# Attention and a gated MLP on one core: W_out read in place, joined groups on TensorE, and matmuls of ones

## The chip, the cores and the metric

The kernel runs on one core of a Trainium2 chip. A core has TensorE (PE, matrix products into PSUM), VectorE (DVE), ScalarE (ACT), GpSimd (POOL) and SyncE (SP, which here only issues transfers). PE's results go to eight PSUM banks of 128 x 512 f32. The metric is the device time of one execution in microseconds; the median of the runs counts.

## The reference

Random-feature attention for 8 batches and 8 heads (576 rows, head size 64, 128 features), then an MLP over all 4608 rows (512 to 2048 to 512).

```
scale = 1.0 / np.sqrt(np.sqrt(D))
def phi(x):
    proj = np.einsum('bhsd,md->bhsm', x, omega)
    sq = np.sum(x * x, axis=-1, keepdims=True) / 2.0
    h = proj - sq
    h = h - np.max(h, axis=-1, keepdims=True)
    return np.exp(h) / np.sqrt(m)
q_p, k_p = phi(q * scale), phi(k * scale)
kv = np.einsum('bhsm,bhsd->bhmd', k_p, v)
num = np.einsum('bhsm,bhmd->bhsd', q_p, kv)
den = np.einsum('bhsm,bhm->bhs', q_p, np.sum(k_p, axis=2))[..., None] + 1e-06
x = num / den                # then heads side by side: 4608 x 512
h = x @ w_in
out = (h * (1.0 / (1.0 + np.exp(-h)))) @ w_out
```

## The kernel before, in words

**Pairs.** Two heads of a batch make a pair; 32 pairs (`NWIN`), numbered n, four to a batch. A pair's 2 x 576 rows are nine chunks of 128: four of each head and a middle chunk of 64 + 64 rows. For keys and queries (`who` is k or q): `project` (L287, eight matmuls of a 64-row half each) and `project_mid` (L294, the middle chunk); `square_sum` (L279); the maxima by `top` (L303, L301); `shift` (L307, L308, the number to be subtracted); then for the first eight pairs (`DIRECT`) nine exponentials `expo` on ACT (L323), and from then on a subtraction on DVE (`lower`) and one exponential of all (`expo_all`, L337). The sum of the keys' features is `zsum_direct` (L358, L360) on PE for the first eight pairs and `sums` on POOL with `zsum` (L352) on PE for the others. `denom` or `denom_direct` (L369, L409) is on DVE, `normal` (L419, three groups of three chunks) on POOL divides the queries' features, `turn` (L425) transposes them on PE, three chunks a time, and `en_copy` (L429) brings them to SBUF. `kv` (L389), `kt_copy`, `kv_turn` (L397) and `kw_copy` make the key-value matrix; `numer` (L443) gives x transposed, and `x_high`, `x_low` (L457, L462) split it into two float32r parts.

**MLP.** A tile t is 512 rows of batch t (tile 8 collects the remaining 64 rows of all eight). It has 16 steps f. `stage1` (L539) does W_in, three products (high-high, low-high, high-low) for each of four k; `silu` and `g_low` split the activation; `stage2` (L557) does W_out into four banks that are held for the whole tile, two steps (`LAG`) behind. A step is 24 matmuls of 128 x 512. The eight banks are four `acc`, two `h` (stage 1) and two `att` (everything of the attention, once the MLP runs).

**Weights.** They arrive as float64 words. Once, in the first tile, ACT (`exponent`) and DVE (`word`, three pieces: L500, L502, L506) make float32 of each block of 128 rows, and POOL splits it (`weight_high` L520, `weight_low` L524). W_in's parts stay in SBUF. W_out's are written by POOL into a ring `wp` of two slots, sent to DRAM by `keep_weight` (L527), and read back into the ring `wo` (three slots) by `get_weight` (L531) for each of the 144 steps, the first tile's too.

**Order.** A planner in Python (`Plan`) sets the order of all instructions on all engines before anything runs. Each unit has an engine, an estimated duration, a due time (`key`), inputs (`after`), rings that it takes slots of, and banks. It walks through estimated time and at each step picks, among the units that could start about now, the one due first. `HANDOFF` is its estimate of the step from one engine to another. `shift_keys` adds random numbers, from the seeds in `SHIFTS`, to the due times before 235, so that the order of the first tile is one draw of many. `LEAD` (4) pairs go ahead of the MLP. Each engine works its own list in order; waits are set where lists depend on each other.

Of the kernel before, what the change touches and what calls it, by code (L numbers as in the profile page):

```python
# [9 lines left out]
F32 = mybir.dt.float32  # L10
# [9 lines left out]
P = 128  # L20
# [26 lines left out]
    "en": 2, "den": 2, "rd": 2, "wraw": 3, "w32": 3, "wre": 2, "wo": 3, "wp": 2, "gh": 3, "gl": 3, "ot": 2,  # L47
# [28 lines left out]
class Plan:  # L76
# [16 lines left out]
    def run(self, until=None):  # L93
# [50 lines left out]
        while any(ready.values()):  # L144
# [75 lines left out]
def attention_mlp(ctx: ExitStack, tc: tile.TileContext, qT, kT, qn, kn, v, om_in, w_in, w_out, out):  # L220
# [175 lines left out]
    def kv_turn(n, ps):  # L396
        nc.tensor.transpose(ps[:, :P], T.pop(("kt", n)), ident)  # L397
        T["kwp", n] = ps

    def kw_copy(n):  # L400
        T["kw", n] = kw = new("kw", [P, P])
        nc.scalar.copy(kw, T.pop(("kwp", n))[:, :P])
# [18 lines left out]
    def turn(n, g, ps):  # L421
        if g == 0:
            T["en", n] = new("en", [P, NC * P])
        for i in range(3):
            nc.tensor.transpose(ps[:, i * P : (i + 1) * P], T["h", n, "q"][:, 3 * g + i], ident)  # L425
        T["t", n, g] = ps

    def en_copy(n, g):
        nc.scalar.copy(T["en", n][:, 3 * g * P : 3 * (g + 1) * P], T.pop(("t", n, g))[:, : 3 * P])  # L429
# [96 lines left out]
    def keep_weight(f):  # L526
        nc.sync.dma_start(wo_d[f].bitcast(F32), T.pop(("wp", f)).bitcast(F32))  # L527
# [64 lines left out]
    for n in range(NWIN):  # L592
        calm = n < LEAD
        for i, who in enumerate("kq"):
# [3 lines left out]
            def prev(s):  # L598
# [18 lines left out]
            add(md, "PE", 0.25, at(n, 3 * i + 0.1, o + 5.2), lambda ps, n=n, who=who: project_mid(n, who, ps),  # L617
                banks=1, after=mid_after, free=[("raw",) + w])
# [50 lines left out]
        add(("ktt", n), "PE", 0.2, at(n, 6.7, 36.5), lambda ps, n=n: kv_turn(n, ps), after=[("kt", n)], banks=1,  # L669
            free=[("kt", n)])  # L670
        add(("kw", n), "ACT", 0.3, at(n, 6.8, 36.7), lambda n=n: kw_copy(n), after=[("ktt", n)], order=[("kw", n - 1)] if n else [],
            alloc=[("kw", ("kw", n))], free=[bk(("ktt", n))])
        if n < DIRECT:
            add(("den", n), "DVE", 2.8, at(n, 8, 34.2), lambda n=n: denom_direct(n), after=e["q"] + [zn],
# [5 lines left out]
        for g in range(3):  # L680
            add(("norm", n, g), "POOL", 0.85, at(n, 9 + 0.1 * g, 37 + 0.1 * g), lambda n=n, g=g: normal(n, g),
                after=[("den", n)], order=[("norm", n, g - 1)] if g else [], free=[("rd", n)])
            add(("turn", n, g), "PE", 0.34, at(n, 9.5 + 0.1 * g, 44.2 + 0.8 * g), lambda ps, n=n, g=g: turn(n, g, ps),
                after=[("norm", n, g)], order=[("turn", n, g - 1)] if g else ([("turn", n - 1, 2)] if n else []),
                alloc=[] if g else [("en", ("en", n))], banks=1, free=[("h", n, "q")])
            add(("en", n, g), "ACT", 0.5, at(n, 9.6 + 0.1 * g, 44.4 + 0.8 * g), lambda n=n, g=g: en_copy(n, g),
                after=[("turn", n, g)], free=[bk(("turn", n, g))])
# [36 lines left out]
    for f in range(NF):  # L724
# [14 lines left out]
    for i, (t, f) in enumerate(steps):  # L739
        key = clock(i)  # L740
        late = i >= total - LAG
        add(("get", t, f), "SP", 0.36, clock(i + LAG - AHEAD_OUT), lambda t=t, f=f: get_weight(t, f),
            after=[("keep", f)], order=[("get",) + divmod(i - 1, NF)] if i else [],
            alloc=[("wo", ("wo", t, f))], lat=2.1)
# [11 lines left out]
        for j in range(4):  # L756
# [4 lines left out]
            w = [("get", t, f)]  # L761
# [64 lines left out]
```

## Time and profile before

| what | us |
|---|---|
| median of three runs (lowest, highest) | 1077.16 (1076.47, 1077.48) |
| the profiled execution, its own time | 1076.36 |
| its span | 1074.6 |
| stage 1, three groups of L539, PE busy | 236.4, 225.3, 225.7 |
| stage 2, two groups of L557, PE busy | 371.0, 226.1 |

The profile page gives busy times of the engines, then the span in 40 slices (a digit is tenths; PEclk is the clock granted to PE), the transfers, a chain of what ended last, and groups of instructions by line. Busy times of PE overlap, since matmuls are pipelined: 1152 matmuls of L557 with a mean of 403 ns start much closer together than that. PEld are PE's weight loads, beside its matmuls. Windows show the same for chosen stretches, with the clock's mean there (1.00 is full), and the waits name the engine that came last.

### The profile page before, as it was taken

To read this page: it belongs to the slowest core of one execution; us is meant where nothing else is said; L and a number is where in the kernel's file an instruction comes from. 1 tells how busy PE (TensorE), PEld (TensorE's weight loads), DVE (VectorE), ACT (ScalarE), POOL (GpSimd) and SP (SyncE) were. 2 spreads that over 40 slices of the span, in tenths; PEclk is the share of its full clock that TensorE was granted. 3 is DMA by queue.
4 is the path that set the end of the run, shared out by engine and by line. 5 is a ranking of instruction groups with operands and counts; after the bars stand their busy time and mean duration, and the time that the engine had idled before them with its cause. 6 is when DMAs were issued, how large, how long until landed. Compare 5 with 4: busy or idle time off the path is not lost.

```text
span 1074.6 us, 16797 instructions
## 1 busy us (share of the span) xinstructions
PE 1046.7 (97%) x6044; PEld 838.8 (78%) x6044; DVE 529.4 (49%) x1573; ACT 572.3 (53%) x1049; POOL 220.4 (21%) x289
## 2 busy tenths in 40 slices
PE   6899999999999999999999999999999999999998
PEld 5667877778777787787777877778778788888886
DVE  7998777655544544555454554445454421111111
ACT  5677875555556655555556555665555433222221
POOL 2444455402222112222202122211222200000000
PEclk8989999999999999999999999999999999999999
DMA  7967877654445443543454434544343226223333
GB/s 278 334 203 234 288 245 251 223 170 124 131 132 172 142 141 121 161 151 111 131 166 149 129 129 134 162 142 143 123 145 94 74 92 198 97 98 136 99 99 98
DMA packets 66530, 167.88 MB, mean 156 GB/s; under 512 B 15632, under 2 KB 15760, under 8 KB 66448
## 3 DMA queue, kind: packets, MB, share of 16 engines
q1 hardware_dynamic: 65984, 166.23, 47.8%
q8 instruction: 48, 0.79, 0.3%
q10 hardware_dynamic: 464, 0.59, 0.1%
q14 instruction: 34, 0.28, 0.1%
HBM read 146.87 MB, written 19.92 MB: 155 GB/s over the span
## 4 chain that ended last, share of the span: by engine, by line
PE 90%; DVE 4%; ACT 2%; DMA 1%; issue 1%; POOL 0%; ACTq 0%; SPq 0%; DVEq 0%
PE ps_acc L557 37%; PE ps_h L539 36%; PE ps_att L287 5%; PE ps_att L389 3%; PE ps_att L425 3%; PE ps_att L443 2%; PE ps_att L294 1%; DVE prod L369 1%; PE ps_att L352 1%; PE ps_att L360 1%; DVE w L502 1%; DMA wo<-wo_d 1%; DMA rawq<-qT 0%; ACT hk L323 0%; PE ps_acc L287 0%
## 5 line engine op out<-in xcount | busy, mean ns | idle before, releaser
L557 PE MATMUL ps_acc<-wo,gh 128*128 128x512 f32 x1152 | 371.0, 403 | 3.2 <-ACT hk L323 1.8
L544 ACT ACTIVATE gh<-ps_h 128x512 fp32r<-128x512 f32 x144 | 86.1, 598 | 308.3 <-PE ps_h L539 297.1
L557 PEld LDWEIGHTS ps_acc<-wo,gh 128*128 128x128 f32 x1152 | 206.2, 189 | 46.0 <-ACT hk L323 2.2
L549 DVE TENSOR_TENSOR gl<-ps_h,gh 128x512 fp32r<-128x512 f32 x144 | 99.2, 689 | 284.4 <-ACT ps_h L545 284.3
L539 PE MATMUL ps_h<-xh,wh 128*128 128x512 f32 x576 | 236.4, 410 | 0.3 <-ACT hk L323 0.3
L539 PE MATMUL ps_h<-xl,wh 128*128 128x512 f32 x576 | 225.3, 391 | 1.5 <-DVE xl L462 1.5
L557 PE MATMUL ps_acc<-wo,gl 128*128 128x512 f32 x576 | 226.1, 393 | 0.0
L539 PE MATMUL ps_h<-xh,wl 128*128 128x512 f32 x576 | 225.7, 392 | 0.0
L419 POOL TENSOR_TENSOR hq<-hq,rd 128x384 f32<-128x384 f32 x96 | 79.2, 852 | 382.5 <-DVE rd L414 173.6
L539 PEld LDWEIGHTS ps_h<-xh,wh 128*128 128x128 f32 x576 | 108.4, 188 | 25.0 <-ACT hk L323 0.5
L539 PEld LDWEIGHTS ps_h<-xh,wl 128*128 128x128 f32 x576 | 108.2, 188 | 23.9
L557 PEld LDWEIGHTS ps_acc<-wo,gl 128*128 128x128 f32 x576 | 108.4, 188 | 23.6
L539 PEld LDWEIGHTS ps_h<-xl,wh 128*128 128x128 f32 x576 | 108.5, 188 | 22.5 <-DVE xl L462 1.8
L544 ACT ACT_TABLE_LOAD x58 | 74.4, 1283 | 36.1 <-PE ps_h L539 35.4
L303 DVE TENSOR_REDUCE mxq<-ps_att 128x4 f32<-128x512 f32 x56 | 36.1, 687 | 100.3 <-PE ps_att L287 100.2
L545 ACT ACTIVATE ps_h<-ps_h 128x512 f32<-128x512 f32 x144 | 85.4, 593 | 0.0
L337 ACT ACT_TABLE_LOAD x48 | 61.6, 1283 | 35.7 <-DVE hq L328 34.3
L343 POOL TENSOR_TENSOR t<-hk 128x256 f32<-128x256 f32 x48 | 34.4, 738 | 199.1 <-ACT hk L337 199.1
L409 DVE CUSTOM_DVE_ANT_0 prod<-hq,zb 128x128 f32<-128x128 f32 x216 | 47.8, 288 | 38.9 <-ACT zb L382 38.9
L303 DVE TENSOR_REDUCE mxk<-ps_att 128x4 f32<-128x512 f32 x55 | 35.6, 687 | 38.3 <-PE ps_att L287 37.8
L275 ACT ACTIVATE nat<-nat 128x576 f32<-128x576 f32 x64 | 44.4, 697 | 14.6 <-DMA nat<-kn 10.5
L429 ACT COPY en<-ps_att 128x384 f32<-128x384 f32 x89 | 40.5, 480 | 7.0 <-PE ps_att L425 5.4
(129 smaller groups left out, 1192.9 us busy)
## 6 DMA issues: line engine op xcount, KB each, us to landing
wo<-wo_d SPq DMA_DIRECT2D x144, 512.0 KB, 3.4
rawk<-kT SPq DMA_DIRECT2D x32, 352.0 KB, 3.0
rawq<-qT SPq DMA_DIRECT2D x32, 352.0 KB, 4.2
v<-v SPq DMA_DIRECT2D x32, 320.0 KB, 3.0
nat<-kn SPq DMA_DIRECT2D x32, 288.0 KB, 3.0
nat<-qn SPq DMA_DIRECT2D x32, 288.0 KB, 3.4
wraw<-w_in SPq DMA_DIRECT2D x16, 512.0 KB, 4.1
wraw<-w_out SPq DMA_DIRECT2D x16, 512.0 KB, 5.0
```

The costliest lines, as they stand in the source:

```text
L275: nc.scalar.activation(nat, nat, AF.Square, scale=SCALE * 0.5**0.5)
L287: nc.tensor.matmul(ps[:, i * M : (i + 1) * M], raw[r, o : o + P], oms[r], start=True, stop=True)
L303: nc.vector.tensor_reduce(m[:, 5 * j : 5 * j + 4], ps.rearrange("p (c m) -> p c m", m=M), AX.X, ALU.max)
L337: nc.scalar.activation(h, h, AF.Exp)
L409: nc.vector.tensor_tensor_reduce(out=prod[:, c], in0=e[:, c], in1=zb[:, j], scale=1.0, scalar=GUARD, op0=ALU.mult, op1=ALU.add, accum_out= ...
L419: nc.gpsimd.tensor_tensor(e[:, c], e[:, c], rd[:, c].unsqueeze(2).broadcast_to([P, 3, M]), ALU.mult)
L429: nc.scalar.copy(T["en", n][:, 3 * g * P : 3 * (g + 1) * P], T.pop(("t", n, g))[:, : 3 * P])
L539: nc.tensor.matmul(ph, w[:, k, :], x, start=k == 0 and n == 0, stop=k == NK - 1 and n == 2)
L544: nc.scalar.activation(gh, ph, AF.Silu)
L545: nc.scalar.activation(ph, ph, AF.Silu)
L549: nc.vector.tensor_tensor(gl, T["ph", t, f], T["gh", t, f].bitcast(F32), ALU.subtract)
L557: nc.tensor.matmul(T["po", t][j], g[:, js], w, start=f == 0 and n == 0, stop=f == NF - 1 and n == 2)
```

## The change

Three things, and the planner's numbers.

W_out in place: the ring `wp` goes, and `wo` has five slots. POOL writes the split of step f into a slot of `wo`; stage 2 of the first tile reads it there, and `keep_weight` sends the same slot to DRAM for later tiles. `get_weight` is issued from the second tile on.

Joined groups: from the ninth pair on (n > `DIRECT`), the middle projection of pair n and a group of three transposes of pair n - 1 are one unit in one bank (`mid_turn`, twice a pair: keys with group 0, queries with group 2), and `zsum` with `kv_turn` is one unit in one bank (`zsum_turn`). Group 1 of the transposes stays alone.

Matmuls of ones: where the planner, before its time 100, sees PE idle for over 1 us ahead of a unit with a bank, it puts `pulses` into the gap, matmuls of ones into the bank that the unit will overwrite. The order has them five times, 5, 6, 8, 7 and 9.

The planner's `HANDOFF` is 0.05 lower for four engines, its estimate of `denom_direct` is 2.6 and not 2.8, and the seeds are others.

```diff
-    "en": 2, "den": 2, "rd": 2, "wraw": 3, "w32": 3, "wre": 2, "wo": 3, "wp": 2, "gh": 3, "gl": 3, "ot": 2,
+    "en": 2, "den": 2, "rd": 2, "wraw": 3, "w32": 3, "wre": 2, "wo": 5, "gh": 3, "gl": 3, "ot": 2,
-HANDOFF = {"PE": 0.3, "ACT": 0.15, "DVE": 0.15, "POOL": 0.2, "SP": 0.2}
+HANDOFF = {"PE": 0.25, "ACT": 0.1, "DVE": 0.1, "POOL": 0.15, "SP": 0.2}
-SHIFTS = (1000, 1001, 1004, 1005, 1007, 1011, 1020, 1026, 1056, 1068, 1094, 1152, 1161,)
+SHIFTS = (3005, 3006, 3008, 3013, 3017, 3024, 3072, 3100, 3183, 3232, 3249, 3387, 3510,)
+HOT = 100.0
+PULSE = 0.24
...
-                if t - free_at[e] > 2.5:
+                idle = t - free_at[e]
+                u["hot"] = 0
+                if u["banks"] and t < HOT and idle > 1.0:
+                    since = max([free_at[e]] + [slot_time(p, pools[:i].count(p)) for i, p in enumerate(pools)])
+                    u["hot"] = max(0, int((t - since - 0.4) / PULSE))
+                    idle -= u["hot"] * PULSE
+                if idle > 2.5:
                     warm = t + 4.0
...
+    def pulses(ps, n):
+        for _ in range(n):
+            nc.tensor.matmul(ps[:, :P], ones, ones, start=True, stop=True)
...
+    def mid_turn(n, who, g, ps):
+        project_mid(n + 1, who, ps)
+        turn(n, g, ps, M)
+
+    def zsum_turn(n, ps):
+        zsum(n, ps)
+        kv_turn(n, ps, 2 * M)
...
-        if ("wp", f) not in T:
-            T["wp", f] = new("wp", [P, 2, DMODEL], F32R)
-        return T["wp", f][:, 0], T["wp", f][:, 1]
+        if ("wo", 0, f) not in T:
+            T["wo", 0, f] = new("wo", [P, 2, DMODEL], F32R)
+        return T["wo", 0, f][:, 0], T["wo", 0, f][:, 1]
...
-        nc.sync.dma_start(wo_d[f].bitcast(F32), T.pop(("wp", f)).bitcast(F32))
+        nc.sync.dma_start(wo_d[f].bitcast(F32), T["wo", 0, f].bitcast(F32))
...
+            if n > DIRECT:
+                md = ("mt", n - 1, 2 * i)
+                waits = mid_after + [("norm", n - 1, 2 * i), ("turn" if i == 0 else "mt", n - 2 + i, 0 if i and n - 2 + i >= DIRECT else 2)]
...
+                add(md, "PE", 0.59, at(n, 0, o + 5.2), lambda ps, n=n, who=who, g=2 * i: mid_turn(n - 1, who, g, ps),
+                    banks=1, after=waits[:-1], order=waits[-1:], alloc=[] if i else [("en", ("en", n - 1))],
+                    free=[("raw",) + w, ("h", n - 1, "q")])
...
+            joined = n > DIRECT
+            add(zn, "PE", 0.7 if joined else 0.5, at(n, 7, 32), lambda ps, n=n, f=zsum_turn if joined else zsum: f(n, ps),
+                after=[("sums", n)] + [("kt", n)] * joined, banks=1, free=[("es", n)] + [("kt", n)] * joined)
...
-            add(("den", n), "DVE", 2.8, at(n, 8, 34.2), lambda n=n: denom_direct(n), after=e["q"] + [zn],
+            add(("den", n), "DVE", 2.6, at(n, 8, 34.2), lambda n=n: denom_direct(n), after=e["q"] + [zn],
...
-            w = [("get", t, f)]
+            w = [("get", t, f)] if t else [("wlo", "out", f)]
...
-            u["fn"](*[bank(p) for p in u["pools"]])
+            ps = [bank(p) for p in u["pools"]]
+            if u.get("hot"):
+                pulses(ps[0], u["hot"])
+            u["fn"](*ps)
```

**Where instructions move: DVE behind the first denominator.** Before: DVE's list from pair 1's sum of squares of the keys (`sqk`) on; `nbk`, `nbq` are the shifts of keys and queries, `w_303` and `w_306` float32 blocks of W_out and W_in.

```order
L279 TENSOR_REDUCE sqk<-nat 128x9
L307 TENSOR_TENSOR nbk<-mxk,sqk 128x9
L308 SCALAR_TENSOR_TENSOR nbk<-nbk,sqk 128x9
L500 TENSOR_SCALAR w_303<-wraw 128x512
L500 TENSOR_SCALAR w_306<-wraw 128x512
L279 TENSOR_REDUCE sqq<-nat 128x9
L502 SCALAR_TENSOR_TENSOR w_306<-wre,w_306 128x512
L506 SCALAR_TENSOR_TENSOR w_306<-wraw,w_306 128x512
L502 SCALAR_TENSOR_TENSOR w_303<-wre,w_303 128x512
L301 TENSOR_REDUCE mxq<-ps_acc 128x1
L307 TENSOR_TENSOR nbq<-mxq,sqq 128x9
L308 SCALAR_TENSOR_TENSOR nbq<-nbq,sqq 128x9
```

After, from the same sum of squares on; the last row is that of pair 2.

```order
L291 TENSOR_REDUCE sqk<-nat 128x9
L319 TENSOR_TENSOR nbk<-mxk,sqk 128x9
L320 SCALAR_TENSOR_TENSOR nbk<-nbk,sqk 128x9
L291 TENSOR_REDUCE sqq<-nat 128x9
L319 TENSOR_TENSOR nbq<-mxq,sqq 128x9
L320 SCALAR_TENSOR_TENSOR nbq<-nbq,sqq 128x9
L526 SCALAR_TENSOR_TENSOR w_248<-wraw,w_248 128x512
L520 TENSOR_SCALAR w_349<-wraw 128x512
L520 TENSOR_SCALAR w_353<-wraw 128x512
L522 SCALAR_TENSOR_TENSOR w_349<-wre,w_349 128x512
L526 SCALAR_TENSOR_TENSOR w_349<-wraw,w_349 128x512
L291 TENSOR_REDUCE sqk<-nat 128x9
```

The shift of the queries (`nbq`) has moved from behind five pieces of weights and a maximum to right behind that of the keys; the weight pieces stand behind both.

**SP in the first 60 us.** Before: SP's list from the second block of W_out that goes to DRAM on (`wo_d` is that copy, `rest` the 64 rows kept for tile 8, `rawk`, `nat`, `v` inputs).

```order
L527 DMA wo_d<-wp 128x1024
L531 DMA wo<-wo_d 128x1024
L479 DMA wraw<-w_out 128x512
L271 DMA v<-v 128x640
L467 DMA rest_90<-xh_526 128x64
L467 DMA rest_94<-xl_527 128x64
L267 DMA nat<-kn 128x576
L531 DMA wo<-wo_d 128x1024
L263 DMA rawk<-kT 128x704
```

After, from the second block of W_out on:

```order
L547 DMA wo_d<-wo 128x1024
L487 DMA rest_90<-xh_582 128x64
L487 DMA rest_94<-xl_583 128x64
L279 DMA nat<-qn 128x576
L279 DMA nat<-kn 128x576
L499 DMA wraw<-w_out 128x512
L279 DMA nat<-qn 128x576
L275 DMA rawq<-qT 128x704
L283 DMA v<-v 128x640
```

The reads `wo<-wo_d` are gone from here, as from the whole first tile; the writes stay, out of the ring `wo`.

**PE in the steady part.** Before: PE's list in a step of a pair past the ninth, from the middle projection (L294) of the next pair's keys on; L557 is stage 2 and L425 transposes of the queries' features.

```order
L294 MATMUL ps_att<-oms,rawk 128x128
L557 MATMUL ps_acc<-wo,gh 128x512 x2
L557 MATMUL ps_acc<-wo,gl 128x512
L425 MATMUL ps_att<-ident,hq 128x128 x3
L557 MATMUL ps_acc<-wo,gh 128x512 x2
L557 MATMUL ps_acc<-wo,gl 128x512
L425 MATMUL ps_att<-ident,hq 128x128 x6
L557 MATMUL ps_acc<-wo,gh 128x512 x2
```

After, at the same place (L306 is the middle projection, L437 transposes, L577 stage 2):

```order
L306 MATMUL ps_att<-oms,rawk 128x128
L437 MATMUL ps_att<-ident,hq 128x128 x3
L577 MATMUL ps_acc<-wo,gh 128x512 x2
L577 MATMUL ps_acc<-wo,gl 128x512
L437 MATMUL ps_att<-ident,hq 128x128 x3
L577 MATMUL ps_acc<-wo,gh 128x512 x2
L577 MATMUL ps_acc<-wo,gl 128x512
```

The middle projection and the first three transposes now follow each other without a stage 2 group between them; the second three stand alone, and the third three have moved behind the middle projection of the next pair's queries.

More of the change, by code (lines that the diff above doesn't have):

```diff
@@ L91, in add, with run @@
             self.freed_by.setdefault(i, []).append(name)
-    def run(self, until=None):
+    def run(self, until=None, heat=None):
         end, first = {}, {}
@@ L394, in kt_copy, with kv_turn @@
         nc.scalar.copy(kt, T.pop(("kv", n))[:, :M])
-    def kv_turn(n, ps):
-        nc.tensor.transpose(ps[:, :P], T.pop(("kt", n)), ident)
-        T["kwp", n] = ps
+    def kv_turn(n, ps, off=0):
+        nc.tensor.transpose(ps[:, off : off + P], T.pop(("kt", n)), ident)
+        T["kwp", n] = ps[:, off : off + P]
     def kw_copy(n):
         T["kw", n] = kw = new("kw", [P, P])
-        nc.scalar.copy(kw, T.pop(("kwp", n))[:, :P])
+        nc.scalar.copy(kw, T.pop(("kwp", n)))
     def denom(n):
@@ L419, in normal, with turn @@
         nc.gpsimd.tensor_tensor(e[:, c], e[:, c], rd[:, c].unsqueeze(2).broadcast_to([P, 3, M]), ALU.mult)
-    def turn(n, g, ps):
+    def turn(n, g, ps, off=0):
         if g == 0:
@@ L424, in turn @@
         for i in range(3):
[L425 to L426 removed]
+            nc.tensor.transpose(ps[:, off + i * P : off + (i + 1) * P], T["h", n, "q"][:, 3 * g + i], ident)
+        T["t", n, g] = ps[:, off : off + 3 * P]
+    def mid_turn(n, who, g, ps):
[4 more added lines that the diff above has]
+        kv_turn(n, ps, 2 * M)
     def en_copy(n, g):
[L429 removed]
+        nc.scalar.copy(T["en", n][:, 3 * g * P : 3 * (g + 1) * P], T.pop(("t", n, g)))
     rest_d = [[dram.tile([P, MAIN], F32R, tag=f"rest{a}{k}", name=f"rest{a}{k}") for k in range(NK)] for a in range(2)]
@@ L668, in attention_mlp @@
             alloc=[("kt", ("kt", n))], free=[bk(kn_, 1 if merged else 0)])
[L669 to L672, printed above, removed]
+        kx = ("ktt", n)
+        if n > DIRECT:
+            kx = zn
+        else:
+            add(kx, "PE", 0.2, at(n, 6.7, 36.5), lambda ps, n=n: kv_turn(n, ps), after=[("kt", n)], banks=1,
+                free=[("kt", n)])
+        add(("kw", n), "ACT", 0.3, at(n, 6.8, 36.7), lambda n=n: kw_copy(n), after=[kx], order=[("kw", n - 1)] if n else [],
+            alloc=[("kw", ("kw", n))], free=[bk(kx)])
         if n < DIRECT:
-            add(("den", n), "DVE", 2.8, at(n, 8, 34.2), lambda n=n: denom_direct(n), after=e["q"] + [zn],
+            add(("den", n), "DVE", 2.6, at(n, 8, 34.2), lambda n=n: denom_direct(n), after=e["q"] + [zn],
                 order=[("den", n - 1)] if n else [], alloc=[("den", ("den", n)), ("rd", ("rd", n))], free=[bk(zn)])
@@ L682, in attention_mlp @@
                 after=[("den", n)], order=[("norm", n, g - 1)] if g else [], free=[("rd", n)])
-            add(("turn", n, g), "PE", 0.34, at(n, 9.5 + 0.1 * g, 44.2 + 0.8 * g), lambda ps, n=n, g=g: turn(n, g, ps),
-                after=[("norm", n, g)], order=[("turn", n, g - 1)] if g else ([("turn", n - 1, 2)] if n else []),
-                alloc=[] if g else [("en", ("en", n))], banks=1, free=[("h", n, "q")])
+            joint = DIRECT <= n < NWIN - 1
+            tu = ("turn", n, g)
+            if joint and g != 1:
+                tu = ("mt", n, g)
+            else:
+                last_turn = ("mt", n - 1, 2) if n > DIRECT else ("turn", n - 1, 2)
+                first_turn = ("mt" if joint else "turn", n, g - 1)
+                add(tu, "PE", 0.34, at(n, 9.5 + 0.1 * g, 44.2 + 0.8 * g), lambda ps, n=n, g=g: turn(n, g, ps),
+                    after=[("norm", n, g)], order=[first_turn] if g else ([last_turn] if n else []),
+                    alloc=[] if g else [("en", ("en", n))], banks=1, free=[("h", n, "q")])
             add(("en", n, g), "ACT", 0.5, at(n, 9.6 + 0.1 * g, 44.4 + 0.8 * g), lambda n=n, g=g: en_copy(n, g),
-                after=[("turn", n, g)], free=[bk(("turn", n, g))])
+                after=[tu], free=[bk(tu)])
         t, k = divmod(n, NPAIR)
@@ L741, in attention_mlp @@
         late = i >= total - LAG
-        add(("get", t, f), "SP", 0.36, clock(i + LAG - AHEAD_OUT), lambda t=t, f=f: get_weight(t, f),
-            after=[("keep", f)], order=[("get",) + divmod(i - 1, NF)] if i else [],
-            alloc=[("wo", ("wo", t, f))], lat=2.1)
+        if t:
+            before = ("get",) + divmod(i - 1, NF) if i > NF else ("wlo", "out", NF - 1)
+            add(("get", t, f), "SP", 0.36, clock(i + LAG - AHEAD_OUT), lambda t=t, f=f: get_weight(t, f),
+                after=[("keep", f)], order=[before], alloc=[("wo", ("wo", t, f))], lat=2.1)
         for k in range(NK):
```

14 lines of the change are left out of this document (9 added, 5 removed).

## The prediction

> **What bounds the kernel now.** I read the page's first part first, then the granted clock by slices, then the windows by stage, the waits of TensorE, and last the timeline of single instructions.
>
> ```profile
> PE 1046.7 (97%) x6044; PEld 838.8 (78%) x6044; DVE 529.4 (49%) x1573; ACT 572.3 (53%) x1049; POOL 220.4 (21%) x289
> PEclk8989999999999999999999999999999999999999
> ```
>
> TensorE (PE) is busy for 97% of the span, and the clock that it is granted is under full only in the first slices, of about 27 us each. A time can fall here in two ways alone: less work on PE, or less waiting and less half clock while PE is not yet full.
>
> ```profile
> 300.00:400.00 100.00, 100.00 (x602) 79.46 (x603) 50.70 (x156) 59.67 (x98) 17.84 (x27) 1.00 0.46 145
> ```
>
> This row of the windows (length, then PE, PEld, DVE, ACT, POOL busy, granted clock, DMA share) is the steady part: PE is never idle, and no other engine is above 60%. The next rows are stretches of the first 200 us, most of them with PE short of full.
>
> ```profile
> 16.60:23.70 7.10, 0.00 (x0) 0.01 (x1) 7.00 (x12) 3.35 (x9) 4.72 (x5) 0.63 0.55 196
> 38.00:47.00 9.00, 8.68 (x89) 7.03 (x86) 8.69 (x28) 7.42 (x25) 3.21 (x4) 1.00 1.02 354
> 53.00:61.00 8.00, 7.93 (x48) 6.26 (x47) 7.19 (x12) 6.41 (x24) 4.21 (x4) 0.60 0.76 243
> 75.20:100.00 24.80, 22.76 (x125) 18.42 (x126) 20.97 (x65) 21.36 (x44) 10.28 (x10) 1.00 0.67 214
> 152.40:160.00 7.60, 5.89 (x29) 4.80 (x30) 5.04 (x11) 7.54 (x16) 2.92 (x4) 0.78 0.77 285
> 169.70:176.00 6.30, 4.29 (x24) 3.00 (x23) 5.03 (x9) 1.76 (x6) 4.35 (x5) 0.73 0.86 283
> ```
>
> From 16.6 to 23.7 PE does nothing while VectorE (DVE) works 7.00 of 7.10 us. From 53 to 61 PE is full but at a clock of 0.60. After 75.2 three stretches are short of full by 2.04, 1.71 and 2.01 us, and in the last two the clock falls too: (1 - 0.78) x 7.6 and (1 - 0.73) x 6.3 are 1.7 us of lost work each. The waits say for whom:
>
> ```profile
> PE ps_h L425 <- ACT hk L323: 7.1, 1, 7.1
> PE ps_acc L425 <- POOL hq L419: 2.1, 3, 1.6
> PE ps_att L397 <- DVE xl L462: 2.0, 1, 2.0
> PE ps_acc L557 <- ACT hk L323: 1.8, 1, 1.8
> PE ps_acc L425 <- ACT hk L323: 1.7, 1, 1.7
> PE ps_acc L557 <- DMA wo<-wo_d: 1.4, 1, 1.4
> ```
>
> Columns are microseconds, times, longest. All of these lie in the first 200 us. The one on L557 for the DMA is stage 2 of the first tile waiting for W_out to come back from DRAM.
>
> **The fill: the order of the first pairs.** The fill is paced by a chain through DVE. Rows of DVE's timeline (start, duration, line, operation, idle time before):
>
> ```profile
> 17.25 0.68 DVE L303 TENSOR_REDUCE mxq<-ps_h 128x4 f32<-128x512 f32 x1
> 17.85 1.28 DVE L502 SCALAR_TENSOR_TENSOR w<-wre,w 128x512 uint32<-128x512 uint32 x1
> 19.16 1.20 DVE L506 SCALAR_TENSOR_TENSOR w<-wraw,w 128x512 uint32<-128x512 uint32 x1
> 20.29 0.74 DVE L279 TENSOR_REDUCE sqk<-nat 128x9 f32<-128x576 f32 x1
> ...
> 21.27 1.14 DVE L308 SCALAR_TENSOR_TENSOR nbk<-nbk,sqk 128x9 f32<-128x9 f32 x1
> 22.32 0.75 DVE L500 TENSOR_SCALAR w<-wraw 128x512 uint32<-128x512 uint32 x2
> ...
> 24.37 0.69 DVE L506 SCALAR_TENSOR_TENSOR w<-wraw,w 128x512 uint32<-128x512 uint32 x1
> ...
> 26.67 0.85 DVE L307 TENSOR_TENSOR nbq<-mxq,sqq 128x9 f32<-128x9 f32 x1
> ...
> 31.27 0.28 DVE L369 CUSTOM_DVE_ANT_0 prod<-hq,ps_acc 128x128 f32<-128x128 f32 x1
> ```
>
> ```profile
> 72.63 0.68 DVE L462 TENSOR_TENSOR xl<-ps_att,xh 128x512 fp32r<-128x512 f32 x1
> ```
>
> In before, the denominator of pair 0 ends at 16.8 us; two weight pieces (1.28 and 1.20) stand ahead of the shift of pair 1's keys (21.27, itself 1.14), and five weight pieces and a wait stand ahead of the shift of its queries (26.67). The denominator of pair 1 starts at 31.27. In the new order one weight piece is left ahead of the keys' shift, and none stands between it and that of the queries. By hand: pair 0 itself comes about 1.3 us later, since two sums of squares and the first maximum of the queries now stand ahead of its shift, and ones are multiplied ahead of its projection. So its denominator ends near 18.1. Then three maxima (1.4), one weight piece (1.2), a sum of squares (0.7) and the shift (0.4) give 21.8; the exponentials of keys and queries on ScalarE (ACT), 2.5 and 2.6 us as before, and one copy of 0.5 give 27.4 against 31.27: a lead of 3.9 us.
>
> From there to the last piece of pair 3's x (L462, ending at 73.3) counts of the two orders give the rest. In all, up to that piece, the new order has two more each of sums of squares, maxima and shifts (+3.3 us by 0.66 and 0.60, the records' 0.74 and 0.68 less the 0.08 by which they overlap, and 0.37) and two fewer L500 and five fewer L502 or L506 (-4.1 us by 0.34 and 0.69): 0.8 us less. Ahead of pair 1's denominator it has one sum of squares more and one L500 and four L502 or L506 fewer, 2.4 us less, so 1.6 us more behind it. The lead at pair 3's x is 3.9 - 1.6 = 2.3 us. By then the new order has also projected one more set of keys on PE, 1.0 us of work that needs no time later. **Fill: -3.3 us.** Bounds: +1.1 (no lead, and the first five matmuls of ones run past the arrival of omega) and -6 (the lead is kept, and the waits of 1.6 and 1.7 near 50 us go too). I take the middle, since the lead is counted but the transfers are not: the DMA engines are full (share 1.02) from 38 to 47 us.
>
> **The matmuls of ones.** Five groups, of 5, 6, 8, 7 and 9, are 35 matmuls of two passes each. A pass is 0.11 us at full clock (L294's 0.23 below is two) and 0.21 at half. They cost nothing where PE would wait anyway, and the 7.1 us, the 1.6, 1.7 and 1.8 us waits above are such places. Without that cover all are 70 x 0.11 = 7.7 us. What they can bring is the clock: 53 to 61 us at 0.60 is 3.2 us of lost work, but DVE is busy 7.19 of 8.00 there, so most of it is not on the path. I count **0**, with 0 to +7.7 against and 0 to -3 for.
>
> **W_out read in place.** In before, the split W_out of step f goes to DRAM and comes back before stage 2 of the first tile can use it. Rows of the DMA answer for 100 to 160 us (count, size, median us from issue to landing):
>
> ```profile
> wo<-wo_d SPq DMA_DIRECT2D x6, 512.0 KB, 5.3
> wo_d<-wp SPq DMA_DIRECT2D x5, 512.0 KB, 5.4
> ```
>
> The round trip is 10.7 us beside queueing. In the new kernel PE waits for GpSimd's second half of the split alone, which is at least that much earlier, so the 1.4 us wait before 155.3 goes with 9 us to spare, and what is late next there is the stage-1 result, a plain step behind. With it goes the idle time that came ahead of the low clock, 1.7 us. **W_out: -3.1 us**, bounds 0 (another wait stands at that place) and -3.1. Sixteen reads of 512 KB leave the queue in the first 200 us as well; the writes stay. Each slot of the ring of five is now held from the split to stage 2; GpSimd's sixth split waits for the first stage 2, which in the orders stands ahead of it by a whole step, so this costs nothing unless PE runs late.
>
> The Trainium skill, "TensorE: Matmul & The Clock Gate", section "Part 1: The HAM clock gate", says that the clock falls after a whole idle window of about 3.4 us. By that rule a wait of 1.4 us would not lower the clock and W_out would bring 1.4, the sum 1.7 us less; the trace differs, since the clock is 0.78 in a stretch whose idle time is 1.71 us in all, so I stay with the row.
>
> **The joined groups.** Three rows of PE each show what one inserted group costs. PE's timeline, from the large matmul ahead to the second one behind:
>
> ```profile
> 304.30 0.39 PE L557 MATMUL ps_acc<-wo,gl 128*128 128x512 f32 x1
> 304.53 0.38 PE L294 MATMUL ps_att<-oms,rawq 128*128 128x128 f32 x2
> 304.67 0.48 PE L539 MATMUL ps_h<-xh,wh 128*128 128x512 f32 x1
> 304.98 0.40 PE L539 MATMUL ps_h<-xl,wh 128*128 128x512 f32 x1
> ```
>
> ```profile
> 323.46 0.40 PE L557 MATMUL ps_acc<-wo,gl 128*128 128x512 f32 x1
> 323.70 0.49 PE L425 MATMUL ps_att<-ident,hq 128*128 128x128 f32 x3
> 323.95 0.71 PE L557 MATMUL ps_acc<-wo,gh 128*128 128x512 f32 x2
> 324.50 0.39 PE L557 MATMUL ps_acc<-wo,gl 128*128 128x512 f32 x1
> ```
>
> ```profile
> 114.07 0.39 PE L539 MATMUL ps_h<-xh,wl 128*128 128x512 f32 x1
> 114.30 0.38 PE L294 MATMUL ps_att<-oms,rawk 128*128 128x128 f32 x2
> 114.52 0.49 PE L425 MATMUL ps_att<-ident,hq 128*128 128x128 f32 x3
> 114.76 0.47 PE L539 MATMUL ps_h<-xh,wh 128*128 128x512 f32 x1
> 115.08 0.39 PE L539 MATMUL ps_h<-xl,wh 128*128 128x512 f32 x1
> ```
>
> Large matmuls start 0.227 us apart. The middle projection alone costs 304.98 - 304.30 - 2 x 0.227 = 0.23; three transposes alone 324.50 - 323.46 - 3 x 0.227 = 0.36; both side by side, which the old order has here by chance, 115.08 - 114.07 - 2 x 0.227 = 0.56. A join saves about 0.03 us. The change makes three joins for each of 23 pairs (two of projection and transposes, one of L352 and L397): 69 x 0.03 = **-2.0 us**, bounds 0 and -4. A joined group waits for both of its inputs, and behind it on PE stands everything else; the last join of a pair needs its copy by ACT before the numerators, which in the new order stand 15 large matmuls (3.4 us) and 1.1 us of other work behind, with ACT at 60%: no wait counted.
>
> **Sum.** -3.3 - 3.1 - 2.0 = -8.4 us against the profiled execution's own 1076.36 us (span 1074.6 and 1.8 around it) is 1068.0; the median of the runs is 0.8 above that execution, so 1068.8.
>
> **Rivals.**
> - Only the counted work moves: the fill's lead is eaten by DVE, which was busy 7.00 of 7.10 us before 23.7 and 7.19 of 8.00 before 61 and has nearly the same work, and by loads. Then -3.1 - 2.0: 1072.1. For it: those shares. Against: two weight pieces left the chain at 17.85. Chance 0.24.
> - The waits only change place: another late piece stands in the first tile where W_out did, as xl did at 172.1 for 2.0 us and a lower clock. Then the joins alone: 1075.2. Chance 0.12.
> - Slower: the ones stand where PE has no gap. The groups of 7 and 9 are ahead of transposes at 47 to 75 us; where the reordered operands are ready earlier than planned, PE works off ones in front of them. All 35 on the path are 7.7 us at full clock and 14.7 at half; with the middle, 11, no gain of the fill, and W_out and the joins as above, the sum is 11 - 5.1 = +5.9: 1083.1. It decides for slower once 5.1 + 2.2 us of them are uncovered. Against: every group is put where before has a long wait nearby. Chance 0.10.
> - The forecast, 1068.8 with 1064 to 1071 around it: 0.54.
>
> **How the numbers follow.** The low end takes fill and joins at their bounds (-6 - 3.1 - 4 is 1064) and 2 us for a steadier clock: 1062. The high end takes in the second rival and a small loss, 1077.5. A measurement of this kernel can tell about 0.2%, 2.2 us, from no change. Faster by more: the forecast, the first rival and some of the second, 0.82; within: 0.08; slower: 0.10.
>
> **What would show it.** Pair 1's denominator on DVE near 27 us and pair 3's last x near 71; no wait on a DMA of wo in the first tile and the clock at 1.00 there; 0.56 us for a middle projection with transposes in the steady part; the ones ending before the operand of the next group comes. A PE idle over 1 us between 80 and 200 us, or transposes starting straight behind ones whose operand was long ready, would make the forecast wrong.

## The result, and the profile after

| | median of the runs, us | all runs, us | ratio to before (95%) |
|---|---|---|---|
| before | 1077.32 | 1076.47 to 1077.66 (4) | |
| after | 1068.45 | 1066.94 to 1070.42 (4) | 0.9924 (0.9910 to 0.9938) |

The change makes the kernel 8.9 us faster; 1068.8 was predicted. The profiled execution of after took 1068.94 us (span 1067.2) against 1076.36 of before, 7.4 us less. The first part and the clock line of its page:

```profile
PE 1048.0 (98%) x6114; PEld 844.1 (79%) x6114; DVE 533.9 (50%) x1573; ACT 571.0 (54%) x1047; POOL 222.4 (21%) x289
PEclk9999999999999999999999999999999999999999
```

TensorE executes 70 more passes than before and is as busy, in a span that is 7.4 us shorter; no slice is under 0.9 of the clock. The windows of after, the stretches that the prediction showed of before and two long ones (start:end, length, then PE, PEld, DVE, ACT, POOL busy, granted clock, DMA share, GB/s):

```profile
16.60:23.70 7.10, 4.24 (x48) 3.20 (x47) 6.80 (x31) 4.09 (x11) 2.85 (x3) 1.00 0.61 187
53.00:61.00 8.00, 7.72 (x85) 6.16 (x83) 6.93 (x26) 7.79 (x27) 3.19 (x4) 1.00 0.87 276
75.20:200.00 124.80, 123.17 (x745) 98.95 (x746) 107.36 (x251) 88.20 (x167) 70.53 (x70) 1.00 0.66 219
152.40:160.00 7.60, 7.60 (x51) 6.51 (x50) 6.29 (x14) 5.28 (x13) 4.86 (x5) 1.00 0.57 228
169.70:176.00 6.30, 6.30 (x40) 4.96 (x39) 5.26 (x12) 2.35 (x5) 2.81 (x4) 1.00 0.70 241
200.00:400.00 200.00, 198.01 (x1182) 157.85 (x1182) 102.43 (x324) 118.08 (x197) 37.88 (x56) 1.00 0.45 142
```

The same two long ones of before:

```profile
75.20:200.00 124.80, 119.01 (x704) 95.07 (x704) 99.62 (x250) 91.12 (x175) 62.45 (x63) 0.97 0.74 244
200.00:400.00 200.00, 200.00 (x1192) 159.18 (x1191) 102.36 (x319) 118.95 (x195) 38.28 (x56) 1.00 0.48 149
```

From 75.2 to 200 us PE lost 5.8 us idle and 3.4 to the clock ((1 - 0.78) x 7.6 and (1 - 0.73) x 6.3, the two stretches that the prediction shows); after loses 1.6 idle and nothing to the clock. That is the larger part of the gain. From 200 to 400 it went the other way: before was never idle there, after is for 2.0 us. The waits of PE in after (microseconds, times, longest):

```profile
PE ps_h L437 <- issue: 1.9, 1, 1.9
PE ps_acc L437 <- POOL hq L431: 1.8, 3, 1.0
...
PE ps_att L306 <- DVE hq L343: 1.1, 1, 1.1
PE ps_att L299 <- DVE xl L482: 1.0, 1, 1.0
PE ps_att L299 <- ACT en L449: 0.9, 1, 0.9
```

The longest is 1.9 us where it was 7.1, and none is on the DMA of wo. Those on L306 and on ACT's en are the two new ones, at 330 and 204 us.

A way to see where a difference arises when two orders put work into different stretches is to read the starts of the same result in both traces. Here it is the n-th result of stage 1 that ScalarE turns into gh (there are 144; 16 to a tile). All runs of the study, starts in us in the profiled execution of each, and the median over its runs (names that end in ot4 have four places for finished output, see below):

| run | n = 0 | n = 16 | n = 32 | n = 112 | median |
|---|---|---|---|---|---|
| before | 75.28 | 201.81 | 316.14 | 893.12 | 1077.3 |
| after | 74.23 | 196.65 | 309.24 | 885.69 | 1068.45 |
| e_in_place | 75.34 | 201.96 | 316.27 | 893.71 | 1077.4 |
| b_round_trip | 74.13 | 210.81 | 324.13 | 900.15 | 1083.4 |
| a_no_ones | 72.78 | 197.99 | 310.57 | 893.71 | 1074.7 |
| c_unjoined | 74.88 | 197.29 | 309.77 | 888.49 | 1072.3 |
| after_again | 72.31 | 194.75 | 307.33 | 883.99 | 1067.5 |
| i_after_ot4 | 74.59 | 197.02 | 308.60 | 882.95 | 1066.1 |
| j_no_ones_ot4 | 73.94 | 197.94 | 309.52 | 883.88 | 1066.8 |
| k_before_ot4 | 74.69 | 202.62 | 317.51 | 893.53 | 1077.0 |
| l_unjoined_ot4 | 74.27 | 196.70 | 308.37 | 884.51 | 1068.2 |
| n_no_seeds_ot4 | 81.89 | 206.59 | 316.57 | 890.87 | 1074.4 |
| h_old_no_seeds_ot4 | 80.00 | 205.01 | 320.87 | 896.91 | 1081.1 |
| p_four_groups_ot4 | 76.80 | 199.23 | 310.80 | 885.77 | 1068.6 |

Of after's 7.4 us, 1.1 are there at n = 0, 5.2 at 16, 6.9 at 32, and only 0.5 more come in the 80 steps up to 112, where the joins should have brought nearly all of their 2.0. The 1.7 us between n = 16 and 32 belong to the first tile too: the joins are not their source, since without them this stretch is as short (111.67 us in l_unjoined_ot4, 111.58 in i_after_ot4), and after starts 14 more of the large matmuls than before between n = 0 and 16, by the records 379 against 365, at 0.227 us each.

### The profile page after: what moved, and what is told of

Same layout as the page of the kernel before. It is cut to its first block, busy times and chain, and to the rows that moved or that the text cites. A ratio compares the mean times of both kernels' runs of the same rounds, so it can differ in the third digit from the quotient of the medians.

```text
span 1067.2 us, 16943 instructions
## 1 busy us (share of the span) xinstructions
PE 1048.0 (98%) x6114; PEld 844.1 (79%) x6114; DVE 533.9 (50%) x1573; ACT 571.0 (54%) x1047; POOL 222.4 (21%) x289
## 4 chain that ended last, share of the span: by engine, by line
PE 88%; DVE 5%; ACT 4%; issue 1%; DMA 1%; POOL 0%; ACTq 0%; SPq 0%; DVEq 0%; POOLq 0%
PE ps_h L559 35%; PE ps_acc L577 35%; PE ps_att L299 5%; PE ps_att L401 3%; PE ps_att L437 2%; PE ps_att L463 2%; DVE prod L381 1%; PE ps_att L306 1%; DMA out<-ot 1%; PE ps_att L364 1%; ACT L564 1%; ACT L349 0%; ACT hk L335 0%; DVE w L522 0%; ACT ot L585 0%
## 5 line engine op out<-in xcount | busy, mean ns | idle before, releaser
L577 PE MATMUL ps_acc<-wo,gh 128*128 128x512 f32 x1152 | 366.2, 399 | 0.0
L577 PEld LDWEIGHTS ps_acc<-wo,gh 128*128 128x128 f32 x1152 | 208.1, 188 | 42.6
L559 PE MATMUL ps_h<-xh,wh 128*128 128x512 f32 x576 | 233.1, 405 | 0.5 <-ACT xh L477 0.5
L577 PE MATMUL ps_acc<-wo,gl 128*128 128x512 f32 x576 | 225.2, 391 | 0.0
L577 PEld LDWEIGHTS ps_acc<-wo,gl 128*128 128x128 f32 x576 | 108.1, 188 | 23.5
```

The source lines that it names most:

```text
L559: nc.tensor.matmul(ph, w[:, k, :], x, start=k == 0 and n == 0, stop=k == NK - 1 and n == 2)
L577: nc.tensor.matmul(T["po", t][j], g[:, js], w, start=f == 0 and n == 0, stop=f == NF - 1 and n == 2)
```

## The experiments

The first set (e, b, a, c) ran on one chip (before: 1076.1 there), the second (after_again, i, j, k) and the third (l, n, h, p) on two others (1076.8 on both). Ratios are to before on the same chip. The texts set off say what was expected before each run.

**W_out in place alone (e_in_place).** Before, its order kept on every engine:

```diff
+        return ring.tile(shape, dtype, tag=tag, name=tag, bufs=5 if tag == "wo" else RINGS[tag])
...
+        if ("wo", 0, f) not in T:
+            T["wo", 0, f] = new("wo", [P, 2, DMODEL], F32R)
+        return T["wo", 0, f][:, 0], T["wo", 0, f][:, 1]
...
     def get_weight(t, f):
+        if t == 0:
+            return
```

> The kernel before, with W_out read in place in the first tile as the only change (five slots, the reads of the first tile gone); every instruction keeps its place on every engine. If W_out in place is what empties the first tile of waits, as the prediction's step has it, the 1.4 us wait on the DMA of wo before 155 and the low clock behind it are gone and the time is 3.1 us lower: near 1074.2. If the gain of the first tile comes from the new order of the other work, the wait on wo goes but the one for ACT's or DVE's piece takes its place, the wait of 2.0 for xl at 172 stays with its half clock, and the time is 1076 to 1077. In neither case does it reach 1070.

Measured: 1077.4, ratio to before 1.0005 (0.9994 to 1.0017). No gain. The waits of PE from 80 to 215 us:

```profile
PE ps_att L397 <- DVE xl L462: 3.0, 1, 3.0
PE ps_att L294 <- ACT hq L323: 1.9, 1, 1.9
PE ps_acc L559 <- ACT hk L323: 1.8, 1, 1.8
```

The wait on the DMA of wo is gone, and with it the 16 reads. In its place PE waits 1.9 us for the next piece (hq of ACT, at 158.8), and the wait for xl behind it grows from 2.0 to 3.0. The DMA was late next to other pieces that were late too.

**The new order with the round trip (b_round_trip).** After, its order kept, the split W_out read back from DRAM into its slot:

```diff
+    def fetch(f):
+        nc.sync.dma_start(T["wo", 0, f].bitcast(F32), wo_d[f].bitcast(F32))
...
+        for n, u in enumerate(plan.run()):
+            for f in [f for f in kept if n >= kept[f] or u["name"] == ("s2", 0, f, 0)]:
+                fetch(f)
+                del kept[f]
+            if u["name"][0] == "keep":
+                kept[u["name"][1]] = n + 27
```

> The changed kernel, order kept, but in the first tile each step's split W_out is read back from DRAM into its own slot, 27 units of the plan after it was written or right ahead of its stage 2, whichever comes first, so that PE waits for the round trip as before. By the prediction's step (round trip of 10.7 us, one wait and its half clock, 3.1 us) it loses 3 us or more: 1071.5 or above, and the waits on the DMA of wo are back; since the new order puts some splits close to their stage 2 (from the tenth step on), several waits of 2 to 6 us and a time of 1075 to 1085 are as likely. If the round trip had been hidden by the order alone, no wait on wo of over 1 us shows and the time is 1068 to 1069.

Measured: 1083.4, ratio 1.0062 (1.0040 to 1.0084): 15 us slower than after. From its waits of PE:

```profile
PE ps_acc L580 <- DMA wo<-wo_d: 9.7, 6, 4.0
```

At n = 0 it stands with after, at n = 16 it is 14.2 us behind: the waits, and the clock that falls with them (0.72 in the mean from 150 to 156 us, 0.57 from 198 to 206). So the two halves belong together. Taken alone, reading in place brings 0, and the new order with its round trip, with the reads at the one place that was tried, loses 7 us against before; together they bring 9. At those six waits the new order leaves no room for a round trip between the split of W_out and its stage 2.

**Without the ones (a_no_ones).** After, order kept:

```diff
-            if u.get("hot"):
-                pulses(ps[0], u["hot"])
```

> The changed kernel without its 35 matmuls of ones (they are no part of the output), all else in the same order. If they cost nothing and bring nothing, as the prediction counts them: 1068 to 1069. If they hold the clock through the first 80 us: half-clock windows come back (the trace of the changed kernel has two ahead of 42 us and none behind, that of the kernel before one at 52.6 too) and the time is 1 to 3 us higher. If the first group, which runs cold from 3.8 to 6.1 us in the way of the first projection of keys, delays the whole chain: the first projection starts near 4.7 instead of 6.1, and the time is up to 1.4 lower, 1067.

Measured: 1074.7, ratio 0.9982 (0.9970 to 0.9993), 6 us slower than after; I had expected 1 to 3 at most. The table puts 1.3 us of that in the first tile. The rest came in the steady part (6.7 us from n = 32 to 112 in the profiled execution, the slowest of its twelve runs, 1076.96), though nothing was changed there. The first step on PE's timeline of a_no_ones (start, duration; idle time before in brackets):

```profile
330.00 0.39 PE L559 MATMUL ps_h<-xh,wl 128*128 128x512 f32 x1
333.15 0.77 PE L306 MATMUL ps_att<-oms,rawq 128*128 128x128 f32 x2 [2.77 <-DVE hq L343]
```

DVE was late because ACT was. ACT's timeline in a_no_ones, at the end of the second tile:

```profile
321.25 0.59 ACT L585 COPY ot<-ps_acc 128x512 f32<-128x512 f32 x1 [0.75 <-DMA out<-ot]
325.57 0.59 ACT L585 COPY ot<-ps_acc 128x512 f32<-128x512 f32 x1 [3.73 <-DMA out<-ot]
326.17 1.28 ACT L349 ACT_TABLE_LOAD   x1
327.47 1.17 ACT L349 ACTIVATE hk<-hk 128x1152 f32<-128x1152 f32 x1
```

The same place in after:

```profile
319.95 0.59 ACT L585 COPY ot<-ps_acc 128x512 f32<-128x512 f32 x1 [0.77 <-DMA out<-ot]
322.50 0.59 ACT L585 COPY ot<-ps_acc 128x512 f32<-128x512 f32 x1 [1.96 <-DMA out<-ot]
323.11 1.28 ACT L349 ACT_TABLE_LOAD   x1
324.40 1.17 ACT L349 ACTIVATE hk<-hk 128x1152 f32<-128x1152 f32 x1
```

A tile's four copies of finished output have two slots (ot). The third and the fourth wait until an earlier store of 256 KB has landed, and behind them in ACT's queue stand exponentials and the silu of stage 1. The wait for one store was 1.8 us longer in one execution than in the other, and nearly the whole of it reached PE (2.77 against 1.05). Behind that stop, and behind a second one of 1.97 us at 575 that follows a copy's wait of 3.46, the clock is down to half (start:end, length, busy times, clock, as above):

```profile
332.56:335.97 3.41, 2.81 (x9) 2.56 (x10) 2.19 (x7) 0.62 (x3) 0.00 (x0) 0.50 0.27 55
574.90:578.31 3.41, 3.41 (x9) 2.64 (x10) 1.78 (x17) 1.11 (x5) 0.00 (x0) 0.50 0.56 172
```

That is the whole of the 6.7 us: from n = 32 to 112 PE waits 5.1 us where it waits 1.5 in after, 3.6 more, and half of the 2.81 + 3.41 us of work at half clock, 3.1, is lost. This chain was in no step of the prediction.

**Without joins (c_unjoined).** After with every joined group taken apart; a table in the kernel (not shown) keeps the due times as the seeds had made them:

```diff
+JOIN = 99
...
-            if n > DIRECT:
+            if n > JOIN:
                 md = ("mt", n - 1, 2 * i)
...
-            joined = n > DIRECT
+            joined = n > JOIN
...
```

> The changed kernel without its joined groups: middle projections, transposes, the sums and the turned key sums stand as units of their own as in the kernel before, with the due times of the joined ones; up to the ninth pair's first middle projection TensorE's order is unchanged. By the prediction's term (69 joins of 0.03 us) it loses 2.0 us: 1070.5. By the two traces, in which a pair's inserted groups take 2.156 us before and 2.124 after, it loses 0.7 us, and if the joined groups' waits at 204 and 330 us (0.9 and 1.1) go with them it is 1 us faster than the changed kernel: 1067.5 to 1069.2.

Measured: 1072.3, ratio 0.9958 (0.9943 to 0.9973), 3.9 us slower than after and slower than either sum had it. Its trace, too, has a stop of 1.65 us on PE (at 687), at the end of the same chain: at 673 a copy waited 2.5 us for a store, the exponentials and the next silu followed late, then xl, then PE. The joins can't be read from this pair of runs: the stores stand over them.

**Four places for the output (after_again, i, j, k).** To take that chain away, every second copy of a tile goes into a slot of the weight words, which are done by then; no instruction changes place:

```diff
-            ot = new("ot", [P, DMODEL])
+            ot = new(("ot", "w32")[j % 2], [P, DMODEL])
```

The changed kernel once more beside them:

> The changed kernel itself, as the control on the chip of the next three runs. In the first set of experiments the same order without ones took 6.2 us longer than the changed kernel had in its own runs, of which the first tile explains 1.3; the rest came in the steady part, where ScalarE waited 3.7 us in place of 2.0 for a store of the output (out<-ot) and TensorE 2.8 in place of 1.1 behind it. If that is the draw of the stores from run to run, this kernel too shows a spread of 3 us or more here, its median is anywhere from 1067 to 1073, and its profile has other waits at other places; if the changed kernel is always 6 us better than the one without ones, its median is 1067 to 1069 again.

> The changed kernel with four places in place of two for the copies of finished output (every second one in a slot of the weight words, which are done by then); order kept. If late stores cause the steady waits, ScalarE's waits on the DMA of out are gone (15.6 us in 11 waits in the changed kernel), TensorE's waits at 204 and 330 us with them, the time is 1 to 2 us under the changed kernel's best runs, near 1066, and the runs lie within 1.5 us. If the waits at 204 and 330 come from the joined groups' double inputs alone, time and spread stay as they are.

> The same four places, without the ones (no part of the output). With the stores' draw gone the difference to the run before this one is what the ones do by themselves. By the two traces up to 300 us it is 1.3 us (the clock of 0.90 to 0.94 in three stretches between 38 and 100 us): near 1067.5. If the ones do something to the steady part too, the 6 us stay: 1072. By the prediction's count it is 0.

> The kernel before with the same four places. Its ScalarE waited 10.7 us in 11 waits for stores, but TensorE had no wait over 1 us behind them between 200 and 860 us, so by its trace it gains under 1 us: 1075.5 to 1076.5. If stores explain a part of the 8.9 us between the two kernels, it gains more than the changed kernel does.

Measured: after_again 1067.5, ratio 0.9914 (0.9900 to 0.9928), runs from 1066.9 to 1069.2. With four places: after (i) 1066.1, ratio 0.9899 (0.9884 to 0.9915), runs from 1065.4 to 1067.6, no closer together than after_again's, against what was expected; without ones (j) 1066.8, 0.9906 (0.9890 to 0.9923); before (k) 1077.0, 1.0002 (0.9991 to 1.0013). Windows of i_after_ot4:

```profile
200.00:400.00 200.00, 200.00 (x1194) 159.77 (x1193) 103.62 (x328) 118.36 (x198) 38.36 (x56) 1.00 0.45 143
400.00:860.00 460.00, 460.00 (x2729) 367.51 (x2728) 235.97 (x746) 265.67 (x442) 85.65 (x126) 1.00 0.43 134
```

PE is never idle from 200 to 860 us; the waits at 204 and 330 are gone. So they came from the stores and not from the joined groups' two inputs. After gains 1.4 us by it (the intervals of the two overlap; the idle time that vanishes is shown), the kernel without ones 7.9, across two chips, and before nothing: from 200 us on its PE had waits of 0.7 and 0.4 us alone. The ones are worth 0.7 us here, within the intervals, and 0.9 in the two traces, constant from n = 16 to 112; two executions of one order, after and after_again, differ by 1.9 us at n = 16, so this is not shown to be more than the draw of the run.

Why the stores came later in the kernel without ones isn't explained. All of its twelve runs on that chip took 1072 to 1077 us; the one that was profiled shows 5.1 us of such waits where after has 1.5. The order is the same but for the ones. after_again speaks against a draw from run to run, since its median is as good as after's; whether stores were slower on that chip was not tried, since after did not run there.

**Joins again, the list of numbers, and the first group of ones (l_unjoined_ot4, n_no_seeds_ot4, h_old_no_seeds_ot4, p_four_groups_ot4; l, n, h and p below).** All four with four places for the output. Run l takes c's edit; runs n and h set `SHIFTS = ()` in after and in before; run p keeps only four groups:

```diff
-            if u.get("hot"):
+            if u.get("hot") and u["name"] != ("proj", 0, "k"):
```

> The changed kernel without joined groups and with the four places for finished output, so that the stores' draw does not stand over the joins (without the four places, 'unjoined' took 1072.3 and its trace had a wait of 1.6 behind a store at 687 us). By the prediction's term the joins are worth 2.0 us: 1068.1 against 1066.1. By the traces' 0.03 us a pair they are worth 0.7: 1066.8. If joined groups cost waits of their own, it is 1 us faster than with joins: 1065.

> The changed kernel with four places and with the list of numbers that displaces due times (SHIFTS) empty: the rules are the new ones (W_out in place, joins, ones, hand-off times), but the planner's order is the plain one. If the new rules themselves bring the first tile's gain, it stays within 2 us of 1066.1. If that gain hangs on the list that the change brings along, waits of 1 to 3 us with half clock behind them stand between 75 and 200 us again, and the time is 1070 to 1077.

> The kernel before with four places and its list SHIFTS empty, the counterpart of the run before this one. The difference of the two is what the new rules bring with no list on either side. If the rules bring the gain (place for the split work since W_out need not make its round trip), the difference is 6 us or more: with the run before at 1068 this one takes 1075 or more. If the list brings it, the two lie within 3 us of each other.

> The changed kernel with four places and without the first of the five groups of ones (5 matmuls, which run cold from 3.8 to 6.1 us and push the first projection of keys from 4.7 to 6.1); ones are no part of the output. If that group only delays the first pair, the fill's chain comes up to 1.4 us earlier and the time is 1064.7 to 1065.5. If the chain waits for the loads instead, 1066 as with it. If the first group warms the clock for the projections, up to 1 us slower: 1067.

Measured: l 1068.2, ratio 0.9926 (0.9912 to 0.9940); n 1074.4, 0.9979 (0.9969 to 0.9989); h 1081.1, 1.0049 (1.0034 to 1.0063); p 1068.6, 0.9925 (0.9912 to 0.9939), above all three times that were expected of it.

The joins: ACT's rows at the 32nd and the 112th result, of i_after_ot4:

```profile
308.60 0.60 ACT L564 ACTIVATE gh<-ps_h 128x512 fp32r<-128x512 f32 x1 [0.29 <-PE ps_h L559]
...
882.95 0.60 ACT L564 ACTIVATE gh<-ps_h 128x512 fp32r<-128x512 f32 x1 [4.42 <-PE ps_h L559]
```

and of l_unjoined_ot4:

```profile
308.37 0.60 ACT L1176 ACTIVATE gh<-ps_h 128x512 fp32r<-128x512 f32 x1 [1.15 <-PE ps_h L1171]
...
884.51 0.60 ACT L1176 ACTIVATE gh<-ps_h 128x512 fp32r<-128x512 f32 x1 [4.42 <-PE ps_h L1171]
```

With joins 574.35 us, without 576.14: 1.79 us for 80 steps, that is 20 pairs with three joins each, 0.03 us a join. That is the prediction's number, once no store stands over it. The other runs with four places agree: 574.36, 574.30 and 574.97 with joins (j, n, p), 576.02 and 576.04 without (k, h). (The medians of l and i, 1068.2 and 1066.1, are of two chips.)

The list: with none on either side the new rules are 6.7 us faster than the old ones (ratio 1.0049 to 0.9979, same chip); 2 of that are the joins, by the rows above. Against k and i, on another chip, the list that each kernel brings is worth 4 us in before and 8 in after. So of the 11.0 us between k and i, 6.7 come with the rules and about 4 from a better list. Which of the rules brings the rest of the 6.7, W_out in place or the planner's other estimates (`HANDOFF`, `denom_direct`), no run separates. From 75.2 to 200 us, run n:

```profile
75.20:200.00 124.80, 121.41 (x718) 96.83 (x719) 102.00 (x244) 88.83 (x164) 65.39 (x65) 0.98 0.64 211
```

run h, and i:

```profile
75.20:200.00 124.80, 116.76 (x700) 92.33 (x700) 101.62 (x247) 88.01 (x164) 64.36 (x66) 0.99 0.73 247
75.20:200.00 124.80, 122.84 (x745) 98.63 (x745) 107.37 (x251) 88.21 (x166) 70.91 (x70) 1.00 0.67 219
```

In this stretch run n loses 3.4 us idle and 2.5 to the clock, h 8.0 and 1.7 (a clock of 0.72 from 145 to 151), i 2.0 and nothing. What run n lacks against i is there mostly at the first result already (81.89 against 74.59): in after the list sorts the fill.

## Why the prediction came out

**The total: right, 0.35 us off, and in good part by luck.** The terms were 3.3 for the fill, 3.1 for W_out and 2.0 for the joins; the table has 1.1 at n = 0, 5.8 from there to 32 and 0.5 in the 80 steps behind, 7.4 in the profiled executions where 8.4 was forecast for them. Errors of opposite sign balanced.

- **W_out, -3.1: the step failed.** It said that behind the 1.4 us wait the stage-1 result is next, "a plain step behind". e_in_place shows the next pieces 1.9 and 3.0 us late. For this part the second rival was right: the waits change place. What W_out in place brings, it brings through the order: the new one loses 15 us with the round trip put back (b_round_trip). The prediction saw the wait that goes, but not that an order without the round trip has room to split W_out later: GpSimd ends the split of the fourth block at 83.2 us in after and at 59.4 in before, while that of the last block ends at 192.9 and 198.5. That the planner finds such an order because of this room, and not because of its other new estimates, is not shown.
- **The first tile as a whole: missing from the sum.** Besides W_out's, two waits of 1.8 and 2.0 us and the half clock behind the second were quoted as rows and then left standing. They went as well: 9.2 us of lost time between 75.2 and 200 became 1.6. I had counted the two orders' instructions only up to pair 3's x, at 73 us.
- **Fill, -3.3: mis-sized.** VectorE's timeline of after, pair 1's first row of the denominator with the sum of squares ahead of it, and pair 3's last piece of x:

```profile
28.89 0.76 DVE L291 TENSOR_REDUCE sqk<-nat 128x9 f32<-128x576 f32 x1 [1.00 <-ACT nat L287]
29.57 0.28 DVE L381 CUSTOM_DVE_ANT_0 prod<-hq,ps_acc 128x128 f32<-128x128 f32 x1
...
71.04 0.82 DVE L482 TENSOR_TENSOR xl<-ps_acc,xh 128x512 fp32r<-128x512 f32 x2 [0.36 <-ACT xh L477]
```

  The denominator came at 29.57 instead of 27.4, 1.7 us ahead of before and not 3.9; the piece of x ended at 71.9, 1.4 ahead and not 2.3. In after_again, the same kernel, these were 28.29 and 69.9, so that the lead is 3.0 and 3.4: the run decides over 1.3 to 2 us of it, by when the clock comes up in the first 8 us (below). In both runs another 1.2 us went where the sum had none: from the end of pair 1's keys' shift to the denominator it counted 5.6 us, and both took 6.8. Pair 2's sum of squares stands ahead of the denominator on VectorE and waits 1.0 us for ScalarE's squares (the first row above). At n = 0 after is 1.1 us ahead, after_again 3.0. Counting VectorE's instructions gave the right sign; what it can't give is a wait of VectorE itself and when PE's clock comes up.
- **Joins, -2.0: right** as a term (0.03 us each in l against i), but in after largely given back: 1.1 and 0.9 us of waits at 330 and 204, behind stores. The prediction counted no wait here because ACT was at 60%; ACT's share says nothing of a copy that holds its queue for 2 us.
- **Ones, 0: nearly right**: 0.7 us for them in j against i, within the intervals. The rival in which they cost time did not come. The group of 9 ends before its operand (the transposes at 75.43 wait another 0.58 us for POOL). The second group does not: in after it ends at 9.43, in j the queries that it stands ahead of were there at 7.87.

Of the signs named: no wait on a DMA of wo and a clock of 1.00 in the first tile came true; the denominator near 27 did not, pair 3's x near 71 did within 1 us. A joined middle projection with transposes costs 0.56 us in the steady part, as said (298.68 - 297.67 - 2 x 0.227 in after). "PE idle over 1 us between 80 and 200 us" would have spoken against the forecast; the longest there is 1.0, for xl at 103.

## What to carry to other kernels

Where a planner sets the order, a removed transfer need not be worth its wait: here it was worth nothing in the old order, and the new order could not do without it. Try the edit with the old order, and the new order without the edit, before putting a number on either, and run both sets of rules without the random list, since a better draw of it can pass for a gain of the edit. Count a late copy on an engine that works its list in order with all that stands behind it: two slots for four stores cost nothing in one order and up to 8 us in another (on two chips), and one line took it away. The version with four places for the output, 1066.1 us, is the fastest of the study.

## What the runs showed of the hardware

**When the clock comes up differs from run to run, and it came later wherever PE idled for 0.6 to 0.8 us ahead of its first projection.** PE's timeline of i_after_ot4 at the start:

```profile
1.06 2.93 PE L259 MATMUL ps_att<-ones 128*128 128x128 f32 x12 [1.06 <-DVE ones L245]
3.78 1.63 PE L263 MATMUL ps_att<-ones 128*128 128x128 f32 x10
...
8.19 1.16 PE L299 MATMUL ps_acc<-oms,rawq 64*128 64x128 f32 x16
```

of after:

```profile
3.78 2.34 PE L263 MATMUL ps_att<-ones 128*128 128x128 f32 x10
```

and of j_no_ones_ot4:

```profile
4.74 0.58 PE L299 MATMUL ps_att<-oms,rawk 64*128 64x128 f32 x1 [0.75 <-ACT oms L269]
...
7.87 2.08 PE L299 MATMUL ps_acc<-oms,rawq 64*128 64x128 f32 x16 [0.32 <-DMA rawq<-qT]
```

The same ten passes of ones take 1.63 us in one execution and 2.34 in another: the clock rose within them in the first and only at 7.2 us in the second. Without the first group of ones PE idles for 0.75 us, and its projections run at half speed (2.08 us for 16 in place of 1.16). By the clock's records the full clock begins between 8.2 and 14.0 us in the seven profiled executions without that group, and between 4.1 and 7.2 in the seven with it; i and p, which differ in that group alone, have 4.5 and 10.4. Run p, which keeps the other four groups, pays for the second at half speed (2.77 us in place of 1.50) and comes 2 us later at n = 0. Whether the first group alone would be better than all five was not tried. The Trainium skill, "TensorE: Matmul & The Clock Gate", section "Part 1: The HAM clock gate", says that the windows run free of the kernel's start, so that the point of warming up differs between runs; these traces agree (4.5 us in after_again and 7.2 in after, the same kernel), with a difference larger than the 0.5 us that the section gives.

**A store of 256 KB took 4.9 us from issue to landing in one execution and 3.2 in another, with the same transfers in the queue in the same order** (a_no_ones and after, near 320 us; the copy behind it waited 3.73 and 1.96 us). The spread of after's runs, 1066.9 to 1070.4, is not shown to come from this: the runs of i, with four places, spread over 2.1 us, those of after_again, with two, over 2.3.
